# Linear attention and a low-rank mixer: two normalisations placed ahead of a low-rank product, and a value cast moved to GpSimd

## The chip, the cores and the metric

The kernel runs on one core of one Trainium2 chip. The metric is the device time of one execution in microseconds (us), given as the median of several executions. Of each kernel one execution is also recorded by the hardware profiler. The profile's own clock starts at the first instruction that it records, and all times of day below ("at 29.16") are counted from there.

## What is computed

The reference takes q, k and v of 8 batches, 8 heads, 576 positions and 64 features per head. It applies linear attention and then a mixer to each batch:

```python
r = np.maximum(x, 0.0)                                   # phi, for q and k
phi = np.concatenate([r * c, r * s], axis=-1)            # c, s: cos and sin of the position
kv  = np.einsum('bhsf,bhsd->bhfd', k_p, v)
z   = np.sum(k_p, axis=2)
x   = np.einsum('bhsf,bhfd->bhsd', q_p, kv) / (np.einsum('bhsf,bhf->bhs', q_p, z)[..., None] + 1e-06)
# heads are put side by side: x is (8, 576, 512)
h   = x.transpose(0, 2, 1) @ U @ V                       # over positions, rank 32
u   = x + h.transpose(0, 2, 1)
out = u + np.maximum(u @ w_ch1, 0.0) @ w_ch2             # 512 -> 2048 -> 512
```

Inputs and outputs are float32; the kernel multiplies in bf16 and accumulates in float32.

## The kernel before

**Tiling.** The 576 positions of a batch are five chunks: chunks 0 to 3 have 128 positions each, in an interleaved order (row p of chunk c is position 4p + c), and chunk 4, the "tail", has the last 64. Two batches share one 128-row tail tile. The order `ORD` (line 562) is tail first: 4, 0, 1, 2, 3.

**Stages of a batch.** `q_prep` and `k_prep` (lines 225 and 231) make the cosine and the sine half of phi, one instruction each for a chunk; the engine of each half is an argument. `qtr_unit` (258) transposes phi(q) on TensorE. `v_prep` and `v_block` (191 and 202) cast v into `v_ext`, which has a column of ones behind each head so that one product gives kv and z. `kv_unit` (237) makes kv of four heads: for each head, one matmul for each of the five chunks, and then a cast. `den_unit` (299) makes the reciprocals of the denominators of four heads, and `xh_unit` (315) the normalised attention of four heads in one chunk: four matmuls and then one multiplication on VectorE that releases the accumulator. `A_unit` (359) makes A = transposed x times U, `u_unit` (375) makes u of one chunk, and `uTd_open`, `uTd_mm` and `uTd_evac` (411 to 434) make the transposed u of 128 features directly: four matmuls with the identity open the accumulator, one matmul "V.A" adds h, and a cast stores it as `uT`. `g1_main` (456) makes one of 16 hidden blocks (four matmuls and a ReLU on ScalarE), and `g2_part` (500) a quarter of an output chunk.

**What sets the order.** The schedule is written by hand (line 57): each engine executes its own instructions in the order in which the program names them, and waits only through semaphores. From line 735 on a list of slots, the hidden and output blocks, is emitted one after the other. `at(j, ...)` (708) hangs more work behind slot j. Batch 0 and batch 1 are written out by hand instead of through `attention_plan`. For them `chain_head` (619) goes from v to the normalised attention of heads 0 to 3, `chain_mid` (636) makes heads 4 to 7, opens the transposed u of features 0 to 255 and completes it (this half needs heads 0 to 3 alone), and `chain_end` (659) does the other 256 features. For batch 0, `fill(n)` is a number of idle "keep-warm" matmuls on zeros (`warm0`, 664). For batch 1, `fill1` (723) puts hidden blocks 8 to 12 and two u chunks of batch 0 in between. Batch 1's chains hang behind slot 7, and its q and k preparation behind slots 0 to 6.

**Buffers.** The accumulators are in PSUM under tags. "o" has two buffers, "g" three, "X" and "T" one each. A new tile waits until the tile that had its buffer has been read. `xt` and `xt1` name the tag of each `xh_unit`: in batch 1 all five use "o", and so do both `u_unit` calls of `fill1`.

**Queues.** All loads of q, k and v go out on SP's queue. The weights go out on POOL's, where they stand in order with POOL's own casts: w1 in quarters of four hidden blocks (`w1_load`, 89), the second at line 684, the third and fourth after slot 2, and w2 in four parts after slot 6. A tiny copy to `mark` ahead of a weight load holds POOL until its source is there: line 717 until batch 1's q tail is transposed, line 719 until the first half of batch 1's v has landed. Line 642 does the like for SP, whose loads for batch 2 follow.

In the head of batch 1, v of heads 0 to 3 is cast by VectorE in three instructions and v of heads 4 to 7 by ScalarE in two.

Of the kernel before, what the change touches and what calls it, by code (L numbers as in the profile page):

```python
# [17 lines left out]
def kernel(  # L18
# [14 lines left out]
    H = 8  # L33
# [9 lines left out]
    TS = 64  # L43
# [5 lines left out]
    def tail(b):  # L49
        lo = TS * (b % 2)  # L50
        return slice(lo, lo + TS)
# [8 lines left out]
    kst, vst, qst, kt, vt, qt = {}, {}, {}, {}, {}, {}  # L60
# [40 lines left out]
    def cast(eng, o, i):  # L101
        if eng is nc.scalar:
            nc.scalar.activation(out=o, in_=i, func=AF.Copy, bias=0.0, scale=1.0)  # L103
        else:
            eng.tensor_copy(out=o, in_=i)  # L105


    V_, A_, G_ = nc.vector, nc.scalar, nc.gpsimd
# [9 lines left out]
        out=iota[:, 0:4], pattern=[[1, 4]], base=0, channel_multiplier=4,  # L118
        allow_small_or_imprecise_dtypes=True,
    )  # L120
    for lo in (0, TS):
        nc.gpsimd.iota(
            out=iota[lo : lo + TS, 4:5], pattern=[[1, 1]], base=512, channel_multiplier=1,
# [11 lines left out]
        out=stU[:, 0:4, :], in_=moe_U[0:512, :].rearrange("(p c) r -> p c r", c=4)  # L135
# [33 lines left out]
    def keep_warm(n, tag, bufs):  # L169
        w_ps = ps.tile([P, 512], FP32, tag=tag, bufs=bufs, name="w_ps")  # L170
        for _ in range(n):
            nc.tensor.matmul(out=w_ps, lhsT=zero[:, 0:P], rhs=zero, start=True, stop=True)  # L172
# [3 lines left out]
    mark = const.tile([TS, 1], FP32)  # L176
# [14 lines left out]
    def v_prep(b, h0=0, h1=H, cs=range(5), engs=None):  # L191
        vx = v_ext[b % 2]
        for n, c in enumerate(cs):
            eng = engs[n] if engs else G_
            if eng is None:
                continue
            if c < 4:
                cast(eng, vx[:, c, h0:h1, 0:D], vst[b][:, h0:h1, c, :])
            else:
                cast(eng, vx[tail(b), 4, h0:h1, 0:D], vt[b][tail(b), h0:h1, :])  # L200

    def v_block(b, h0, h1, c0, c1, eng):
        cast(
            eng,
            v_ext[b % 2][:, c0:c1, h0:h1, 0:D].rearrange("p c h d -> p h c d"),
            vst[b][:, h0:h1, c0:c1, :],
        )
# [29 lines left out]
    def kv_unit(b, hg, tag, bufs, eng=None):  # L237
        if b not in kv_sb:
            kv_sb[b] = pool.tile([P, H, E], BF16, tag="kv", bufs=2, name="kv")
        acc = ps.tile([P, 4, E], FP32, tag=tag, bufs=bufs, name="kv_ps")  # L240
        vx = v_ext[b % 2]
        for i in range(4):
            h = hg * 4 + i
            for c in range(5):
                nc.tensor.matmul(  # L245
                    out=acc[:, i, :],
                    lhsT=k_p[b][:, c, h, :] if c < 4 else k_tl[:, h, :],
                    rhs=vx[:, c, h, :],
                    start=(c == 0),
                    stop=(c == 4),  # L250
                )
        cast(eng or V_, kv_sb[b][:, hg * 4 : hg * 4 + 4, :], acc)
# [32 lines left out]
    def qT_of(b, c, h):  # L285
        return q_pT[b][:, c, h, :] if c < 4 else q_tlT[:, h, :]

    def x_alloc(b):
        if b not in x_bf:
            x_bf[b] = pool.tile([P, 4, DM], BF16, tag="x_bf", bufs=2, name="x_bf")  # L290

    def x_of(b, c, rows=slice(0, P)):
        return x_bf[b][:, c, :] if c < 4 else x_tl[rows, :]
# [21 lines left out]
    def xh_unit(b, c, h0, h1, rec, tag, bufs):  # L315
        x_alloc(b)
        n = h1 - h0
        rows = slice(0, P) if c < 4 else tail(b)
        acc = ps.tile([P, n, D], FP32, tag=tag, bufs=bufs, name="xh_ps")
        for h in range(h0, h1):  # L320
            nc.tensor.matmul(
                out=acc[:, h - h0, :], lhsT=qT_of(b, c, h), rhs=kv_sb[b][:, h, 0:D],
                start=True, stop=True,
            )
        nc.vector.tensor_tensor(
            out=x_of(b, c, rows)[:, h0 * D : h1 * D].rearrange("p (i d) -> p i d", d=D),
            in0=acc[rows],
            in1=rec[rows, c, :].unsqueeze(2).to_broadcast([P if c < 4 else TS, n, D]),
            op=ALU.mult,
        )  # L330
# [25 lines left out]
    def U_of(b, c):  # L356
        return U_bf[:, c if c < 4 else 4 + b % 2, :]

    def A_unit(b, tag, bufs, eng=None, n0=0, n1=DM, a_ps=None):
        if b not in A_sb:  # L360
            A_sb[b] = pool.tile([P, DM], BF16, tag="A_sb", bufs=2, name="A_sb")
        if a_ps is None:
            a_ps = ps.tile([P, DM], FP32, tag=tag, bufs=bufs, name="a_ps")
        for c in range(5):
            nc.tensor.matmul(  # L365
                out=a_ps[:, n0:n1],
                lhsT=U_of(b, c),
                rhs=x_of(b, c)[:, n0:n1],
                start=(c == 0),
                stop=(c == 4),  # L370
            )
        cast(eng or V_, A_sb[b][:, n0:n1], a_ps[:, n0:n1])
        return a_ps

    def u_unit(b, c, tag, bufs):
        if b not in u_bf:
            u_bf[b] = pool.tile([P, 4, DM], BF16, tag="u_bf", bufs=3, name="u_bf")
            if b % 2 == 0:
                u_tl[b // 2] = pool.tile([P, DM], BF16, tag="u_tl", bufs=2, name="u_tl")
        rows = slice(0, P) if c < 4 else tail(b)  # L380
        va = ps.tile([P, DM], FP32, tag=tag, bufs=bufs, name="va_ps")
        nc.tensor.matmul(out=va, lhsT=V_bf[:, c, :], rhs=A_sb[b], start=True, stop=True)  # L382
        nc.vector.tensor_tensor(  # L383
            out=u_bf[b][:, c, :] if c < 4 else u_tl[b // 2][rows, :],
            in0=x_of(b, c, rows),
            in1=va[rows, :],
            op=ALU.add,
        )
# [37 lines left out]
    def uTd_evac(b, d, eng):  # L426
        cast(eng, uT[b][:, :, d, :], uT_ps[b, d])

    def uTd_mm(b, d):
        t = uT_ps[b, d]  # L430
        nc.tensor.matmul(
            out=t.rearrange("m c t -> m (c t)"), lhsT=A_sb[b][:, d * P : d * P + P],
            rhs=V_bf[:, 0:4, :].rearrange("r c t -> r (c t)"), start=False, stop=True,
        )
# [127 lines left out]
    ORD = (4, 0, 1, 2, 3)  # L562
# [53 lines left out]
    TL = (0, 1, 2, 3, 4)  # L616
    O2, G3 = ("o", 2), ("g", 3)

    def chain_head(b, fill, xt, engs):
        v_prep(b, 0, 4, (4,), (engs[0],))  # L620
        v_block(b, 0, 4, 0, 3, V_)
        v_block(b, 0, 4, 3, 4, engs[0])
        kv_unit(b, 0, "T", 1)
        fill(0)
        rec0 = den_unit(b, 0, 4, "X", 1)
        v_prep(b, 4, 8, (4,), (A_,))
        v_block(b, 4, 8, 0, 4, A_)
        fill(1)
        for n, c in enumerate(ORD):
            xh_unit(b, c, 0, 4, rec0, *xt[n])  # L630
            if n == 1:
                fill(2)
            if n == 3:
                kv_unit(b, 1, "T", 1, A_)

    def chain_mid(b, fill, xt, dt):
        fill(3)
        m = 3 if b == 0 else 2
        rec1 = den_unit(b, 4, 8, *dt)
        if b == 1:  # L640

            nc.sync.dma_start(out=mark2, in_=rec1[0:1, 0, 0:1])
        for n, c in enumerate(ORD[:m]):
            xh_unit(b, c, 4, 8, rec1, *xt[n])
        u01 = ps.tile([P, 2, 512], FP32, tag="X", bufs=1, name="u01")
        uTd_open(b, 0, None, None, u01[:, 0, :].rearrange("p (c t) -> p c t", c=4))
        uTd_open(b, 1, None, None, u01[:, 1, :].rearrange("p (c t) -> p c t", c=4))
        a0 = A_unit(b, "T", 1, A_, 0, 256)
        fill(4)
        uTd_mm(b, 0)  # L650
        uTd_mm(b, 1)
        uTd_evac(b, 0, A_)
        uTd_evac(b, 1, A_)
        for n, c in enumerate(ORD[m:]):
            xh_unit(b, c, 4, 8, rec1, *xt[m + n])
        fill(5)
        return a0

# [21 lines left out]
    G_.tensor_copy(out=mark, in_=kt[0][0:TS, 0, 0:1])  # L680
    w1_load(0)
    cast_uv()
    chain_head(0, warm0, (O2, O2, G3, G3, O2), (A_,))
    w1_load(1)
    alloc_q(1)
    load_main(qst[1], q, 1)
# [21 lines left out]
    def at(j, *thunks):  # L708
        beside.setdefault(j, []).extend(thunks)
# [6 lines left out]
        at((4, 5, 5, 6, 6)[n], lambda c=c, n=n: k_prep(1, c, (V_, A_)))  # L716
    at(2, lambda: G_.tensor_copy(out=mark, in_=q_tlT[0:TS, 0, TS : TS + 1]))
    at(2, lambda: [w1_load(2), w1_load(3)])
    at(6, lambda: G_.tensor_copy(out=mark, in_=vst[1][0:TS, 0, 0, 0:1]))
    at(6, lambda: [w2_load(n) for n in range(4)])  # L720
    st1 = {}

    def fill1(n):
        if n in (0, 4):
            u_unit(0, 4 if n == 0 else 0, "o", 2)
        if n > 0:
            g1_main(0, 7 + n)

    xt1 = (O2, O2, O2, O2, O2)
    at(7, lambda: chain_head(1, fill1, xt1, (V_,)))  # L730
    at(7, lambda: st1.update(a=chain_mid(1, fill1, xt1, ("T", 1))))
    at(7, lambda: chain_end(1, st1["a"]))
    at(13, lambda: uTd_close(1, 2, V_), lambda: uTd_close(1, 3, A_))
# [2 lines left out]
    for pr in range(NPAIR):  # L736
        e, o = 2 * pr, 2 * pr + 1
# [57 lines left out]
```

## Time and profile before

| | us |
|---|---|
| median of 4 runs | 332.02 |
| lowest and highest of them | 330.39, 334.46 |
| the profiled execution's own time | 331.94 |
| its span, from first to last instruction | 330.2 |
| TensorE busy | 315.5 |
| ScalarE busy | 163.6 |
| VectorE busy | 152.2 |
| GpSimd busy | 30.3 |

The span is what the profile shows, and the 1.7 us between it and the execution's own time lie around it. The mean granted clock of TensorE is 0.999 of full speed. In the profile PE is TensorE, PEld its weight loads, DVE VectorE, ACT ScalarE, POOL GpSimd and SP the engine that issues most loads. A row of the timeline gives start, length, engine, line, operation, tiles and count; the bracket at its end is the time for which the engine stood idle before it and what ended that idle time. Matmuls overlap: one of 512 columns lasts 0.38, but the next starts 0.216 after it, so the cost of a matmul to TensorE is read from start to start. A row with a count merges several instructions.

### The profile page before, as it was taken

How to read it: one execution, taken by the hardware profiler on the slowest of the kernel's cores; microseconds unless marked ns; L12 is line 12 of the kernel's file. 1: busy time of each engine (PE TensorE's matmuls, PEld its weight loads, DVE VectorE, ACT ScalarE, POOL GpSimd, SP SyncE). 2: the span in 40 equal slices, each digit the busy share in tenths (PEclk: the TensorE clock that was granted, in tenths of full speed). 3: DMA queues.
4: the chain of work that ended last, by engine and by line, in shares of the span. 5: the costliest groups of instructions: out<-in, count | busy, mean ns of one | idle time of the engine just before them, and what ended most of it. 6: DMA issues, size and time to landing. Idle time of an engine off the chain costs nothing.

```text
span 330.2 us, 5833 instructions
## 1 busy us (share of the span) xinstructions
PE 315.5 (96%) x2422; PEld 169.1 (51%) x2422; DVE 152.2 (46%) x334; ACT 163.6 (50%) x272; POOL 30.3 (9%) x61
## 2 busy tenths in 40 slices
PE   8899799999889799999999999999999999999995
PEld 3565564485455344556455444556455444464443
DVE  7668754834656951154726940345626610001211
ACT  4828755786819226565900766556700067650000
POOL 1224203001011100000111010000112100000000
PEclk9999999999999999999999999999999999999999
DMA  7999999966344128960499479801552230001131
GB/s 233 272 275 271 207 256 327 283 204 233 106 146 116 46 79 187 238 214 11 115 226 363 150 202 247 268 2 41 151 144 66 79 95 2 0 2 64 64 97 64
DMA packets 79052, 50.73 MB, mean 154 GB/s; under 512 B 47186, under 2 KB 76242, under 8 KB 79026
## 3 DMA queue, kind: packets, MB, share of 16 engines
q1 hardware_dynamic: 72594, 39.09, 42.5%
q0 software_dynamic: 6432, 11.27, 13.5%
q8 instruction: 19, 0.31, 0.4%
q14 instruction: 7, 0.06, 0.1%
HBM read 36.86 MB, written 9.44 MB: 140 GB/s over the span
## 4 chain that ended last, share of the span: by engine, by line
PE 66%; DVE 5%; issue 1%; ACT 1%; DVEq 0%
PE o_ps L518 30%; PE g_ps L466 25%; PE gt_ps L486 3%; PE va_ps L382 2%; PE kv_ps L245 2%; PE x_ps L339 2%; DVE k_p L213 2%; PE a_ps L365 2%; DVE o_sb L528 1%; PE t_ps L262 1%; DVE k_tl L213 1%; DVE rec L297 0%; ACT k_p L211 0%; DVE x_bf L349 0%; DVE rec L296 0%
## 5 line engine op out<-in xcount | busy, mean ns | idle before, releaser
L466 PE MATMUL g_ps<-uT,w_bf 128*128 128x512 bf16 x512 | 118.5, 379 | 0.6 <-DMA w_bf<-in_moe_w_ch_dram 0.6
L518 PE MATMUL o_ps<-w_bf,hid 128*128 128x512 bf16 (+1 forms) x528 | 118.2, 372 | 0.5 <-DVE o_sb L528 0.5
L475 ACT ACTIVATE hid<-g_ps 128x512 bf16<-128x512 f32 x128 | 76.2, 596 | 83.3 <-PE g_ps L466 83.3
L518 PEld LDWEIGHTS <-hid 128*128 128x128 bf16 x528 | 49.9, 98 | 53.6 <-issue 1.6
L466 PEld LDWEIGHTS <-w_bf 128*128 128x128 bf16 x512 | 48.4, 98 | 55.0 <-DMA w_bf<-in_moe_w_ch_dram 0.8
L528 DVE TENSOR_TENSOR o_sb<-u_bf,o_ps 128x512 f32<-128x512 bf16 (+1 forms) x33 | 22.0, 668 | 67.9 <-PE o_ps L518 67.8
L538 POOL DMA_DIRECT2D out_dram<-o_sb x24 | 13.4, 557 | 177.9 <-DVE o_sb L528 160.8
L383 DVE TENSOR_TENSOR u_bf<-x_bf,va_ps 128x512 bf16<-128x512 bf16 x32 | 21.9, 686 | 10.2 <-PE va_ps L382 10.2
L105 DVE CAST kv<-kv_ps 128x260 bf16<-128x260 f32 x14 | 6.0, 428 | 37.1 <-PE kv_ps L245 37.1
L211 ACT ACTIVATE q_p<-qst,sinw 128x512 bf16<-128x512 f32 x29 | 20.4, 710 | 4.0 <-DMA qst<-in_q_dram 3.9
L349 DVE TENSOR_TENSOR x_bf<-x_ps,rec 128x512 bf16<-128x512 f32 x24 | 16.6, 691 | 0.8
L103 ACT ACTIVATE v_ext<-vst 128x512 bf16<-128x512 f32 (+2 forms) x23 | 14.8, 653 | 2.7 <-DMA vst<-in_v_dram 2.6
L486 PE MATMUL gt_ps<-uT_tl,w_bf 128*128 128x128 bf16 x256 | 16.1, 219 | 0.0
L486 PEld LDWEIGHTS <-w_bf 128*128 128x128 bf16 x256 | 15.1, 98 | 1.4
L382 PE MATMUL va_ps<-A_sb,V_bf 128*128 128x512 bf16 x40 | 15.2, 379 | 0.3 <-DVE A_sb L105 0.3
L518 PE MATMUL o_ps<-w_bf,hid_tl 128*128 128x512 bf16 x64 | 15.4, 379 | 0.0
L245 PEld LDWEIGHTS <-k_p 128*128 128x128 bf16 x256 | 11.3, 97 | 6.1 <-ACT k_p L211 2.0
L245 PE MATMUL kv_ps<-v_ext,k_p 128*128 128x65 bf16 x256 | 12.0, 193 | 2.4 <-DVE v_ext L105 2.4
L172 PE MATMUL w_ps<-zero 128*128 128x512 bf16 x40 | 11.9, 433 | 1.8 <-DVE halfpi L142 1.2
L213 DVE TENSOR_SCALAR k_p<-kst,cosw 128x512 bf16<-128x512 f32 x28 | 13.1, 484 | 1.0 <-DMA kst<-in_k_dram 0.9
L339 PEld LDWEIGHTS <-q_pT 128*128 128x128 bf16 x192 | 9.1, 98 | 8.2 <-DVE x_bf L349 1.6
L296 DVE TENSOR_SCALAR rec<-x_ps 128x8 f32<-128x8 f32 (+1 forms) x30 | 4.9, 164 | 17.0 <-PE x_ps L339 16.9
(100 smaller groups left out, 262.0 us busy)
## 6 DMA issues: line engine op xcount, KB each, us to landing
qst<-in_q_dram SPq DMA_DIRECT2D x8, 1024.0 KB, 9.1
kst<-in_k_dram SPq DMA_DIRECT2D x8, 1024.0 KB, 7.8
vst<-in_v_dram SPq DMA_DIRECT2D x6, 1024.0 KB, 9.5
out_dram<-o_sb POOLq DMA_DIRECT2D x24, 256.0 KB, 2.7
w_bf<-in_moe_w_ch_dram POOLq DMA_DIRECT2D x8, 512.0 KB, 10.1
vst<-in_v_dram SPq DMA_DIRECT2D x4, 512.0 KB, 8.2
out_dram<-o_sb SPq DMA_DIRECT2D x7, 256.0 KB, 2.3
qt<-in_q_dram SPq DMA_DIRECT2D x8, 128.0 KB, 8.0
```

Of the source, the lines that this page charges most:

```text
L211: nc.scalar.activation(out=o, in_=i, func=AF.Relu, bias=0.0, scale=w)
L213: eng.tensor_scalar(out=o, in0=i, scalar1=0.0, scalar2=w, op0=ALU.max, op1=ALU.mult)
L245: nc.tensor.matmul(out=acc[:, i, :], lhsT=k_p[b][:, c, h, :] if c < 4 else k_tl[:, h, :], rhs=vx[:, c, h, :], start=(c == 0), stop=(c == 4),)
L339: nc.tensor.matmul(out=acc[:, g, i * E : i * E + E], lhsT=qT_of(b, c, h), rhs=kv_sb[b][:, h, :], start=True, stop=True,)
L349: nc.vector.tensor_tensor(out=x_of(b, c, rows).rearrange("p (g i d) -> p g i d", g=2, d=D), in0=view[:, :, :, 0:D], in1=rec[rows].unsqueez ...
L382: nc.tensor.matmul(out=va, lhsT=V_bf[:, c, :], rhs=A_sb[b], start=True, stop=True)
L383: nc.vector.tensor_tensor(out=u_bf[b][:, c, :] if c < 4 else u_tl[b // 2][rows, :], in0=x_of(b, c, rows), in1=va[rows, :], op=ALU.add,)
L466: nc.tensor.matmul(out=g_ps.rearrange("p (c t) -> p c t", c=4), lhsT=w1_bf[:, d, j * P : j * P + P], rhs=uT[b][:, :, d, :], start=(d == 0) ...
L475: nc.scalar.activation(out=hid[b][:, j, :], in_=g_ps, func=AF.Relu, bias=0.0, scale=1.0)
L486: nc.tensor.matmul(out=g_ps[:, jj, :], lhsT=w1_bf[:, d, j * P : j * P + P], rhs=uT_tl[pr][:, d, :], start=(d == 0), stop=(d == 3),)
L518: nc.tensor.matmul(out=o[:, cols], lhsT=lhs[:, j, c * P : c * P + P], rhs=w2_bf[:, j, cols], start=(j == 0), stop=(j == NJ - 1),)
L528: nc.vector.tensor_tensor(out=o_sb[:, cols], in0=u[:, cols], in1=o[:, cols], op=ALU.add)
```

## The change

There are four edits. In `chain_mid`, two of the remaining `xh_unit` calls (chunks 2 and 3 in batch 0, where m is 3, and chunks 1 and 2 in batch 1, where m is 2) are emitted ahead of `fill(4)` and of the two V.A products, and the rest stay behind them. In batch 0 the second evacuation of transposed u goes from ScalarE to VectorE. In batch 1, v of heads 0 to 3 and the whole v tail are cast by GpSimd, behind the weight loads of slot 2, and the copy to `mark` at line 719 goes. The `u_unit` of `fill1(4)` takes a "g" buffer instead of an "o" buffer, and two keep-warm matmuls come ahead of batch 1's head.

```diff
-    def chain_head(b, fill, xt, engs):
-        v_prep(b, 0, 4, (4,), (engs[0],))
-        v_block(b, 0, 4, 0, 3, V_)
-        v_block(b, 0, 4, 3, 4, engs[0])
+    def chain_head(b, fill, xt):
+        if b == 0:
+            v_prep(b, 0, 4, (4,), (A_,))
+            v_block(b, 0, 4, 0, 3, V_)
+            v_block(b, 0, 4, 3, 4, A_)
         kv_unit(b, 0, "T", 1)
         fill(0)
         rec0 = den_unit(b, 0, 4, "X", 1)
-        v_prep(b, 4, 8, (4,), (A_,))
+        if b == 0:
+            v_prep(b, 4, 8, (4,), (A_,))
         v_block(b, 4, 8, 0, 4, A_)
...
         a0 = A_unit(b, "T", 1, A_, 0, 256)
+        for n in (m, m + 1):
+            xh_unit(b, ORD[n], 4, 8, rec1, *xt[n])
         fill(4)
         uTd_mm(b, 0)
         uTd_mm(b, 1)
         uTd_evac(b, 0, A_)
-        uTd_evac(b, 1, A_)
-        for n, c in enumerate(ORD[m:]):
-            xh_unit(b, c, 4, 8, rec1, *xt[m + n])
+        uTd_evac(b, 1, V_ if b == 0 else A_)
+        for n in range(m + 2, 5):
+            xh_unit(b, ORD[n], 4, 8, rec1, *xt[n])
         fill(5)
...
-    chain_head(0, warm0, (O2, O2, G3, G3, O2), (A_,))
+    chain_head(0, warm0, (O2, O2, G3, G3, O2))
...
     at(2, lambda: [w1_load(2), w1_load(3)])
-    at(6, lambda: G_.tensor_copy(out=mark, in_=vst[1][0:TS, 0, 0, 0:1]))
+    at(2, lambda: v_prep(1, 0, H, (4,), (G_,)))
+    at(2, lambda: v_block(1, 0, 4, 0, 4, G_))
     at(6, lambda: [w2_load(n) for n in range(4)])
...
         if n in (0, 4):
-            u_unit(0, 4 if n == 0 else 0, "o", 2)
+            u_unit(0, 4 if n == 0 else 0, *(O2 if n == 0 else G3))
...
-    at(7, lambda: chain_head(1, fill1, xt1, (V_,)))
+    at(7, lambda: keep_warm(2, "X", 1))
+    at(7, lambda: chain_head(1, fill1, xt1))
```

## The prediction, made before the result

> **What bounds the kernel now.** I read the page first, then the timeline of 16 to 48 us, the only stretch that the diff touches, and last the waits of TensorE behind it.
>
> ```profile
> PE 315.5 (96%) x2422; PEld 169.1 (51%) x2422; DVE 152.2 (46%) x334; ACT 163.6 (50%) x272; POOL 30.3 (9%) x61
> ```
>
> TensorE is busy for 96% of the span; 14.7 us are left in all (330.2 - 315.5). The edit removes no matmul (it adds two idle ones), so it can only gain where TensorE waits inside the stretch. The timeline of TensorE alone, columns start, length, engine, line, operation, tile, count, wait before it:
>
> ```profile
> 20.89 0.60 PE L431 MATMUL u<-V_bf,A_sb 128*128 128x512 bf16 x2 [0.26 <-ACT A_sb L103]
> 21.34 0.42 PE L321 MATMUL xh_ps<-kv,q_pT 128*128 128x64 bf16 x8
> ...
> 22.02 0.72 PE L365 MATMUL a_ps<-x_bf,U_bf 128*128 128x256 bf16 x4
> ...
> 29.16 1.04 PE L466 MATMUL g_ps<-uT,w_bf 128*128 128x512 bf16 x4 [0.64 <-DMA w_bf<-in_moe_w_ch_dram]
> ```
>
> Three things: V.A waits for the cast of A (20.89); the last two normalisations of batch 0 follow it; and at 29.16 TensorE waits for weights. That is the second quarter of w1 (hidden block 4 is the first to read it), issued at 17.91, with its last piece landing at 29.10 in the trace. Then the start of batch 1:
>
> ```profile
> 33.94 1.32 ACT L211 ACTIVATE k_p<-kst,sinw 128x512 bf16<-128x512 f32 x2
> 34.46 0.96 DVE L105 CAST v_ext<-vst 128x768 bf16<-128x768 f32 x2
> ...
> 35.18 0.49 PE L245 MATMUL kv_ps<-v_ext,k_p 128*128 128x65 bf16 x4 [1.50 <-DVE v_ext L105]
> ```
>
> The reader is to see two ends close together: VectorE's v casts end at 35.42 (34.46 + 0.96) and ScalarE's sine halves of k at 35.26 (33.94 + 1.32; single record 35.25). The wait of 1.50 is put down to the first, but the second is nearly as late. Last, batch 1's first half of features:
>
> ```profile
> 42.73 0.42 DVE L325 TENSOR_TENSOR x_bf<-xh_ps,rec 128x256 bf16<-128x256 f32 x1
> 42.76 0.38 PE L382 MATMUL va_ps<-A_sb,V_bf 128*128 128x512 bf16 x1
> ...
> 44.59 1.22 DVE L325 TENSOR_TENSOR x_bf<-xh_ps,rec 128x256 bf16<-128x256 f32 x3 [0.74 <-PE xh_ps L321]
> 45.07 0.29 PE L321 MATMUL xh_ps<-kv,q_pT 128*128 128x64 bf16 x4 [0.39 <-DVE x_bf L325]
> ...
> 46.05 0.60 PE L365 MATMUL a_ps<-x_bf,U_bf 128*128 128x256 bf16 x4
> ```
>
> The third head product at 45.07 needs one of the two "o" buffers and waits until a normalisation frees it. From 45.2 to about 87 TensorE runs without such waits; the later ones (89.5, 93, 112, 116 us) are queues of ACT and DVE that were themselves fed by TensorE, with no DMA named. So what is gained at 45 should reach the end one for one.
>
> **Batch 0, moved normalisations.** Two groups of 4 head products (the x8 at 21.34, 0.25 us of issue) go into the gap before V.A. A's last matmul issues at 20.15, then the products to 20.5, one idle matmul to 20.72; V.A still waits for the A cast and stays at 20.89. Behind it the products' 0.25 is gone. Their "o" and "g" buffers are free (the tail's normalisation ends at 20.08). VectorE, free at 20.74, does the two normalisations at 0.38 each by 21.5, so A's second half no longer waits between its chunks 2 and 3 (0.23 between those two issues where 0.11 is normal: 0.12). Gain here 0.25 + 0.12 = **0.37**. The second uT evacuation moves from ScalarE (0.59) to VectorE (0.69, the row at 23.98), 21.54 to 22.23; behind it VectorE has A's second cast, ready only at about 22.6, so nothing waits. TensorE reads uT at about 22.75, when the first w1 quarter (landed 22.21) is in too.
>
> But this 0.37 ends at 29.16. The w1 quarter comes at 29.10 whatever TensorE did: its issue at 17.91 stands before the edited code, so 0.64 becomes about 1.0. I book **0**; its other end is the full -0.37, if that landing were not last. One thing starts earlier: the mark that reads q_tlT and the w1 quarters 3 and 4 behind it on POOL's queue, 27.22 to about 26.85. They are first needed at 37.17, so no gain; they can take bandwidth from batch 1's k and v, at most those 0.37. VectorE's k_tl waits for kt until 29.91, and 0.28 follows before it is next needed: 0 to +0.1, I take 0.
>
> **Batch 1, v on GpSimd.** Off VectorE: three casts, 33.83 to 35.42. Off ScalarE: the tail's second half (0.42 at 35.76), after kv has begun, 0 on the path. On POOL, behind w1's issues (end 28.92): the 64x512 tail and one 128x1024 block, in place of a 0.39 mark.
>
> ```profile
> 31.54 0.39 POOL L719 COPY mark<-vst 64x1 f32<-64x1 f32 x1 [2.62 <-DMA vst<-in_v_dram]
> 31.99 3.34 POOL L97 DMA_DIRECT2D w_bf<-in_moe_w_ch_dram  x4
> ...
> 55.51 2.29 POOL L105 CAST v_ext<-vst 128x512 bf16<-128x512 f32 x4 [2.30 <-DMA vst<-in_v_dram]
> ```
>
> The tail lands at 30.41 and costs 0.61 (row at 52.59), to 31.06. The first half of v lands at 31.42; by the last line 512 elements cost 0.57 back to back, so 1024 cost 1.15: 31.5 to about 32.7. The Trainium skill, "GPSIMD Engine Reference", section 3.1, gives 1.8 cycles per element at 1.2 GHz, which would make 1.54 and 33.1. Either end is ahead of TensorE, which comes at 33.51. Behind the cast on POOL wait only the four w2 issues: 31.99 becomes about 32.7, landing from about 41 and not read before 71.
>
> So the wait goes over to ScalarE, not away. In the record, kv's chunk 3 loaded its weights at 35.30, right after k's last sine (35.25), and its matmul issued at 35.47, after the last v cast. Now it issues at about 35.33: **-0.14**. It cannot be more, since ScalarE runs without a gap from 30.23, when it got hidden block 4, that is from the w1 landing: 0.60, k_tl 0.72, hidden 5, two sines, hidden 6, two sines. The two keep-warm matmuls (0.43) lie in TensorE's gap from 33.51 to 35.33; without it they would cost 0.43.
>
> **A rule against this part.** VectorE makes k's cosines while POOL casts:
>
> ```profile
> 31.40 0.88 DVE L213 TENSOR_SCALAR k_p<-kst,cosw 128x512 bf16<-128x512 f32 x2
> ```
>
> That is 0.40 from start to start for 512 elements. The Trainium skill, "SBUF — State Buffer", section "Who interferes with whom", says that tensor_scalar, copy and cast on VectorE can run in a mode that takes a port pair shared with GpSimd, and that whoever is second stands still for the whole instruction. Nothing in this trace has a POOL cast beside such an instruction; beside POOL's w2 issues one cosine took 0.61 in place of 0.48. By the row, VectorE loses about 0.13; by the rule up to the cast's 1.15. Cosines end at 33.80, so 35.0 at worst, still ahead of 35.25: the sum is the same by both, 0. The cover is 1.45 us.
>
> **Batch 1, moved normalisations.** After A's first half (last issue 42.64, next slot 42.755) come the products of chunks 1 and 2. Chunk 1 takes the buffer of the tail, normalised by 42.70: it issues at 42.77 to 42.89. Chunk 2 takes that of chunk 0, normalised until 43.15: it issues at 43.21. A **new wait** of 0.33, with u's first V.A, hidden block 11 and the two V.A of features queued behind it. The old one goes: 8 products from 44.26 end their issue at 44.51, the next came at 45.07, so 0.56 saved; chunk 3 now meets a buffer freed at 43.6. A's second half starts at 46.05 - 0.56 + 0.35 (0.33 and two hand-overs of 0.01) = 45.84, and chunk 3's normalisation ends at about 45.6. u moves to the "g" buffers: VectorE frees that one at about 44.7, wanted at 47. ScalarE's hidden block 11 and both evacuations come 0.6 later, 46.3 at the last; the uT tile is read at about 50. Gain **0.21**; ends 0.1 and 0.35, as the new wait is longer by one VectorE step or half gone.
>
> **Sum.** -0.14 - 0.21 = -0.35, against the profiled execution's own 331.94 us (span 330.2 and 1.7 around it): 331.59, so **331.6 us**. That execution is 0.08 below the median 332.02; the four runs lie between 330.39 and 334.46, so this gain is smaller than their spread. About 1% (3.3 us) is what a measurement of this kernel can tell from no change.
>
> **Rivals.**
> B: batch 0 counts as well, because w1's second quarter is in before TensorE asks for it. For: most of its pieces land by 27.3, only stragglers at 28.15 and 29.10. Against: 0.64 of wait in this record. Then 331.6 - 0.4 = 331.2.
> C: the batch 1 move does nothing; the buffer wait only changes its place, 0.56 against 0.56, if chunk 2's product waits for one more normalisation. For: two "o" buffers stay two. Against: chunk 0's normalisation is already running when it is asked for. 331.94 - 0.14 = 331.8.
> D, on the other side: the port pair at the cosines. If POOL's tail (0.61) and block (1.15) both stop VectorE, and w2's issues slow the last two cosines by 0.13 to 0.3 each, the last ends at 33.80 + 1.76 + 0.5 = 36.1, and kv's chunk 3 issues 0.65 later than now: 331.94 + 0.65 - 0.21 = 332.4. It decides once VectorE slips by 1.9 us (35.47 + 0.21 - 33.80). For: POOL's cast and the cosines start within 0.1 of each other. Against: the tail's cast ends before the first cosine.
>
> **How the numbers follow.** Likeliest (A) 0.50, B 0.17, C 0.13, D 0.12, something that this profile does not show 0.08 (of it 0.03 beyond 1% faster, 0.05 beyond 1% slower). A's own range, with the ends of its terms and the medians' scatter, is 331.0 to 332.3. B to D lie between 331.2 and 332.4; with some 0.8 of scatter of such a median on either side the range is 330.4 to 333.1. All four cases are within 1%: faster 0.04, same 0.90, slower 0.06.
>
> **What would show it.** Right, if: kv_ps of batch 1 waits for ScalarE's k_p or VectorE's, no longer for a v_ext cast, and its fourth matmul comes 0.1 to 0.2 earlier relative to the w1 landing; the w_bf wait grows from 0.64 to about 1.0; TensorE shows a wait of about 0.3 for x_bf before u's V.A and none before chunk 3; POOL's cast of 1024 takes 1.1 to 1.6. Wrong, if: the w_bf wait stays or goes (B), cosines of over 1 us stand beside POOL's cast (D), or anything after 50 us changes by more than its shift.

## The result and the profile after

| | before | changed |
|---|---|---|
| median, us | 331.92 (64 executions) | 330.75 (43) |
| lowest and highest | 330.27, 335.87 | 329.48, 334.03 |
| span of the profiled execution | 330.2 | 328.2 |

The ratio is 0.9962, 95% interval 0.9947 to 0.9976: 0.8 to 1.8 us less, 1.3 at the middle. The forecast was 0.35 less. The sign was right, and the time lies inside the stated range, but that is owed to the width of the range (330.4 to 333.1, with the scatter of a median in it): the gain is more than three times the forecast. So the question is where the other 0.9 us comes from. A first hint is that the gain is not even. A tenth of the executions lie below 330.43 before and below 329.78 after, 0.65 less; a tenth lie above 333.90 before and above 331.75 after, 2.15 less.

The two records alone do not answer it. Their spans differ by 2.0, of which 0.6 is there at the first "A" of batch 0 (20.15 against 19.56), ahead of every edit: the first loads came earlier in that execution. From there on I compare distances. The busy times of the page of the changed kernel are nearly those of before:

```profile
PE 315.2 (96%) x2424; PEld 169.4 (52%) x2424; DVE 151.9 (46%) x332; ACT 162.2 (49%) x270; POOL 31.2 (10%) x62
```

TensorE at the end of batch 0, in the changed kernel's timeline:

```profile
19.56 0.27 PE L365 MATMUL a_ps<-x_tl,U_bf 128*128 128x256 bf16 x1
19.67 0.41 PE L321 MATMUL xh_ps<-kv,q_pT 128*128 128x64 bf16 x8
...
20.31 0.61 PE L431 MATMUL u<-V_bf,A_sb 128*128 128x512 bf16 x2
...
21.18 0.60 PE L365 MATMUL a_ps<-x_bf,U_bf 128*128 128x256 bf16 x4
...
21.73 0.61 PE L417 MATMUL uT_ps<-ident,x_bf 128*128 128x128 bf16 x8
...
27.46 1.03 PE L466 MATMUL g_ps<-uT,w_bf 128*128 128x512 bf16 x4
```

and the first and the last of these places before:

```profile
20.15 0.27 PE L365 MATMUL a_ps<-x_tl,U_bf 128*128 128x256 bf16 x1
...
22.69 0.61 PE L417 MATMUL uT_ps<-ident,x_bf 128*128 128x128 bf16 x8
```

The eight products stand ahead of V.A. From V.A to A's second half it is 0.87 (20.31 to 21.18), where it was 1.13. From the last matmul of A's first half to the opening of the next accumulators it is 2.17 (19.56 to 21.73), where it was 2.54: 0.37 less. The wait for w1's second quarter, 0.64 before, is not there at 27.46: in this execution the quarter had landed by 27.1. Then the start of batch 1, all engines:

```profile
30.33 1.72 DVE L213 TENSOR_SCALAR k_p<-kst,cosw 128x512 bf16<-128x512 f32 x2
...
30.72 1.05 POOL L105 CAST v_ext<-vst 128x1024 bf16<-128x1024 f32 x1 [0.46 <-DMA vst<-in_v_dram]
...
32.23 1.32 ACT L211 ACTIVATE k_p<-kst,sinw 128x512 bf16<-128x512 f32 x2
...
32.57 1.00 DVE L213 TENSOR_SCALAR k_p<-kst,cosw 128x512 bf16<-128x512 f32 x2
...
33.18 0.19 PE L245 MATMUL kv_ps<-v_ext,k_p 128*128 128x65 bf16 x1 [0.71 <-DVE k_p L213]
33.45 0.58 ACT L475 ACTIVATE hid<-g_ps 128x512 bf16<-128x512 f32 x1
33.68 0.10 PEld L245 LDWEIGHTS <-k_p 128*128 128x128 bf16 x1 [0.44 <-ACT k_p L211]
33.71 0.19 PE L245 MATMUL kv_ps<-v_ext,k_p 128*128 128x65 bf16 x1 [0.34 <-DVE k_p L213]
```

kv now waits for k alone: VectorE's cosines end at 33.57 and ScalarE's sines at 33.55, nearly at the same moment. And two cosines took 1.72 together while GpSimd cast, where they took 0.88 before. Last, TensorE at batch 1's first half of features:

```profile
40.99 0.29 PE L321 MATMUL xh_ps<-kv,q_pT 128*128 128x64 bf16 x4
41.45 0.29 PE L321 MATMUL xh_ps<-kv,q_pT 128*128 128x64 bf16 x4 [0.17 <-DVE x_bf L325]
41.57 0.38 PE L382 MATMUL va_ps<-A_sb,V_bf 128*128 128x512 bf16 x1
41.79 1.02 PE L466 MATMUL g_ps<-uT,w_bf 128*128 128x512 bf16 x4
42.65 0.59 PE L431 MATMUL u<-V_bf,A_sb 128*128 128x512 bf16 x2
43.08 0.29 PE L321 MATMUL xh_ps<-kv,q_pT 128*128 128x64 bf16 x4
```

The new wait is there (40.99 + 0.13 of issue to 41.45: 0.33, as forecast), and the old one, at the third product (43.08), is gone.

### The profile page after: what moved, and what is told of

Same layout as the page of the kernel before. It is cut to its first block, busy times and chain, and to the rows that moved or that the text cites. A ratio compares the mean times of both kernels' runs of the same rounds, so it can differ in the third digit from the quotient of the medians.

```text
span 328.2 us, 5835 instructions
## 1 busy us (share of the span) xinstructions
PE 315.2 (96%) x2424; PEld 169.4 (52%) x2424; DVE 151.9 (46%) x332; ACT 162.2 (49%) x270; POOL 31.2 (10%) x62
## 4 chain that ended last, share of the span: by engine, by line
PE 67%; DVE 5%; issue 1%; ACT 1%; DVEq 0%
PE o_ps L518 30%; PE g_ps L466 25%; PE gt_ps L486 3%; PE va_ps L382 2%; PE kv_ps L245 2%; PE x_ps L339 2%; DVE k_p L213 2%; PE a_ps L365 2%; DVE o_sb L528 1%; PE t_ps L262 1%; DVE k_tl L213 1%; DVE rec L297 0%; ACT k_p L211 0%; DVE x_bf L349 0%; DVE rec L296 0%
## 5 line engine op out<-in xcount | busy, mean ns | idle before, releaser
L213 DVE TENSOR_SCALAR k_p<-kst,cosw 128x512 bf16<-128x512 f32 x28 | 14.1, 517 | 0.1
L262 PE MATMUL t_ps<-ident,q_p 128*128 128x128 bf16 x128 | 9.6, 219 | 3.4 <-ACT q_tlT L103 1.6
```

Source lines behind the costliest of these rows:

```text
L213: eng.tensor_scalar(out=o, in0=i, scalar1=0.0, scalar2=w, op0=ALU.max, op1=ALU.mult)
```

## The experiments

My first theory after the result, T, was that the wait for w1 belongs to some executions only, and that without it VectorE's v casts end well behind ScalarE's sines, so that moving them is worth 0.5 or more. Its rivals were R, the prediction's own sum, and S, that the gain sits in executions with late loads. These letters are not those of the prediction's rivals. Each part was then run alone. "Before" stands for the kernel before on the same chip.

**The v cast alone** (e1: all edits for batch 1's v and the two keep-warm matmuls, `chain_mid` as before).

```diff
+        if b == 0:
+            v_prep(b, 0, 4, (4,), (A_,))
...
-    at(6, lambda: G_.tensor_copy(out=mark, in_=vst[1][0:TS, 0, 0, 0:1]))
+    at(2, lambda: v_prep(1, 0, H, (4,), (G_,)))
+    at(2, lambda: v_block(1, 0, 4, 0, 4, G_))
...
+    at(7, lambda: keep_warm(2, "X", 1))
```

> Only batch 1's v cast moves to GpSimd (with the keep-warm pair). Theory T (the wait for w1's second quarter at 29.16 belongs to some executions only; without it VectorE's k cosines and v casts, not ScalarE's sines, end last before batch 1's kv): -0.5 to -0.65 us, so a median near 331.3, and in the profile VectorE ends its cosines no more than 0.2 before or after the sines. Rival R (the record of before is typical, ScalarE's sines end last): -0.14, near 331.8. Rival S (the gain sits in executions whose v lands late): nearly the whole -1.2, mostly in the slow half of the runs.

Median 331.73 against 332.39, ratio 0.9968 (0.9948 to 0.9987). Most of the whole gain is here, and R's 0.14 is outside the interval (0.4 to 1.7 less). In its record the sines end last (34.55), the cosines 0.33 earlier. The middle, 1.06, is more than T's 0.5 to 0.65, but T's size is inside the interval.

**Batch 0's part alone** (e2).

```diff
+        early = 2 if b == 0 else 0
+        for n in range(m, m + early):
+            xh_unit(b, ORD[n], 4, 8, rec1, *xt[n])
         fill(4)
         uTd_mm(b, 0)
         uTd_mm(b, 1)
         uTd_evac(b, 0, A_)
-        uTd_evac(b, 1, A_)
-        for n, c in enumerate(ORD[m:]):
-            xh_unit(b, c, 4, 8, rec1, *xt[m + n])
+        uTd_evac(b, 1, V_ if b == 0 and early else A_)
+        for n in range(m + early, 5):
+            xh_unit(b, ORD[n], 4, 8, rec1, *xt[n])
```

> Only batch 0's two normalisations go ahead of V.A, with the second evacuation on VectorE. T: -0.31 where TensorE does not wait for w1's second quarter, 0 where it does, so -0.1 to -0.31; the profile shows A's second half 0.3 to 0.4 earlier relative to A's first half. R: 0, the w1 wait grows by what was gained. S: 0.

Ratio 0.9997 (0.9962 to 1.0031): no gain seen, as R had it. Its record shows where the gain went, first on TensorE:

```profile
28.83 1.04 PE L466 MATMUL g_ps<-uT,w_bf 128*128 128x512 bf16 x4 [1.03 <-DMA w_bf<-in_moe_w_ch_dram]
```

and then on VectorE, in the same record:

```profile
30.49 0.49 DVE L213 TENSOR_SCALAR k_tl<-kt,cosw 64x512 bf16<-64x512 f32 x1 [1.96 <-DMA kt<-in_k_dram]
```

The wait for w1 is 1.03 in place of 0.64, longer by about the 0.37 that was gained, and behind it VectorE waits 1.96 for k's tail.

**Batch 1's part alone** (e3: as e2, with this instead).

```diff
+        early = 2 if b == 1 else 0
...
-            u_unit(0, 4 if n == 0 else 0, "o", 2)
+            u_unit(0, 4 if n == 0 else 0, *(O2 if n == 0 else G3))
```

> Only batch 1's two normalisations go ahead of V.A, with u of batch 0 in a g buffer. T, R and S alike: -0.21, with a new wait of about 0.2 to 0.3 for x_bf ahead of u's product and none ahead of the third head product.

Ratio 0.999 (0.9958 to 1.0021), too wide for 0.2. The records decide: from kv's fourth matmul in batch 1 to the end of the span it is 294.70, 294.72, 294.70, 294.75 and 294.74 us in the five records without this edit (before, e1, e4, f2, f4), and 294.49 to 294.54 in the seven with it and without a fall of the clock (the changed kernel, e3, k2, k3, e6, f6, f1). That is 0.20 less, and each group lies within 0.05.

**No wait for w1** (e4: the kernel before, but hidden blocks 4 to 7 of batch 0 read w1's first quarter, so those values are not the reference's; the loads stay).

```diff
-                lhsT=w1_bf[:, d, j * P : j * P + P],
+                lhsT=w1_bf[:, d, (j % 4 if b == 0 and 4 <= j < 8 else j) * P :][:, 0:P],
```

> The kernel before, with hidden blocks 4 to 7 of batch 0 reading w1's first quarter in place of the second (their values are not the reference's); all loads stay. This takes the w1 wait away. R: TensorE is up to 0.6 earlier at block 4, but VectorE's casts then end last, so -0.2 to -0.4. T: the wait is rare, so the median moves by less than 0.2, and the profile shows kv's fourth matmul waiting for v_ext by about 0.6 more than for k_p.

Ratio 1.0015 (0.9987 to 1.0043). The wait for w1 was 0.64 in the record of before and is found in ten of the fourteen records of all kernels (0.23 to 1.11), but no gain is seen from taking it away. The record shows one reason: VectorE and ScalarE then wait for k's tail, until 29.93, where VectorE started on it at 29.91 before. So a gain ahead of this point has two loads to pass. The median is not clean, though, as the table below shows: without the wait more executions lose their clock, and those without such a loss (330.85 against 331.12, 8 and 26 executions) leave room for a small gain. T's first half falls (the wait is not rare); its second half stands: in this record the v casts end at 34.83 and the sines at 34.33.

**What the record of e2 showed.** Its granted clock was not 1. Two stretches of its trace follow; the columns are start and end, length, the busy time and count of PE, PEld, DVE, ACT and POOL, the granted clock, the DMA share and GB/s:

```profile
32.40:35.80 3.40, 1.50 (x18) 0.71 (x17) 2.98 (x7) 3.38 (x7) 3.35 (x5) 0.99 1.23 214
35.80:39.20 3.40, 2.88 (x39) 1.72 (x37) 1.56 (x4) 1.14 (x2) 0.28 (x1) 0.50 1.24 206
```

and the same two stretches of the kernel before:

```profile
32.40:35.80 3.40, 1.85 (x20) 0.96 (x19) 2.96 (x6) 3.38 (x7) 2.93 (x4) 1.00 1.24 208
35.80:39.20 3.40, 3.10 (x52) 1.87 (x49) 2.29 (x6) 2.06 (x3) 0.00 (x0) 1.00 1.24 206
```

For 3.4 us, right at batch 1's kv, TensorE ran at half its clock. The hidden block there, four matmuls, shows it:

```profile
37.45 1.86 PE L466 MATMUL g_ps<-uT,w_bf 128*128 128x512 bf16 x4
```

It took 1.86 in place of 1.02. Over a span of 330 us, 3.4 us at half make a mean clock of 0.995, and the mean clock is listed for every execution. So each kernel has a share of executions with such a fall, which I count as a mean under 0.9965 (profiled executions are in the counts):

| kernel | with a fall | median without | median with |
|---|---|---|---|
| before (three chips) | 74 of 129 | 331.12, 330.90, 331.74 | 333.15, 332.81, 333.56 |
| changed | 7 of 44 | 330.45 | 331.62 |
| e1, v cast and two keep-warm | 5 of 22 | 331.40 | 332.41 |
| e2, batch 0 only | 8 of 14 | 331.08 | 333.00 |
| e3, batch 1 only | 6 of 14 | 330.79 | 332.98 |
| e4, no wait for w1 | 14 of 22 | 330.85 | 334.06 |

A mean of 0.990 or less is two falls or more: 8 of e4's 22, and 7 of the 59 of before on its chip. In e1 the executions without a fall are no faster than those of before on its chip (331.40 against 331.12). Its gain is in the slow part of the executions, where falls and, by S, late loads both are.

That made theory C (of the clock; not the prediction's rival C): TensorE's gap ahead of batch 1's kv makes the clock fall, and the two keep-warm matmuls, which I had booked at nothing, prevent it.

**The two matmuls alone, and all but them** (k1: the kernel before with this one line; k2: the changed kernel without it).

```diff
+    at(7, lambda: keep_warm(2, "X", 1))
     at(7, lambda: chain_head(1, fill1, xt1, (V_,)))
```

> The kernel before with nothing but the two keep-warm matmuls ahead of batch 1's head. Theory C (clock: TensorE's gap before batch 1's kv, 1.5 to 2.3 us, makes its granted clock fall to half for 3.4 us in about half of the executions of before, at some 2 us each; the two matmuls prevent most of this): the share of executions with a mean clock under 0.9965 falls from about 0.56 (33 of 59) to 0.2 to 0.3, and the median by 0.5 to 1.0 us; executions at full clock are not changed. Rival T (VectorE's v casts end last, and the clock has no part): 0, the matmuls lie in a gap.

> The changed kernel without the two keep-warm matmuls. C: the share of executions under 0.9965 rises from 0.16 (7 of 44) to 0.4 or more, and the median rises by 0.4 to 0.8 us against the changed kernel, so a ratio to before of about 0.998 to 0.999. T: no change, the ratio stays near 0.996.

k1: 6 of 12 with a fall, ratio 0.9995 (0.9961 to 1.0028). k2: 6 of 12, ratio 0.9979 (0.995 to 1.0009). C as I had put it is half wrong: the two matmuls do not do it in the kernel before. The record of k1 shows why, TensorE:

```profile
33.12 0.38 PE L172 MATMUL w_ps<-zero 128*128 128x512 bf16 x1
34.87 0.49 PE L245 MATMUL kv_ps<-v_ext,k_p 128*128 128x65 bf16 x4 [1.37 <-DVE v_ext L105]
...
36.90 1.87 PE L466 MATMUL g_ps<-uT,w_bf 128*128 128x512 bf16 x4
```

1.37 us of the gap stay empty, another 0.30 before the denominators, and the clock falls at 36.5. In the changed kernel the rest of the gap is broken up, since v is there early and kv's first two matmuls run at 32.24. But k2 says that this too is not enough without the two matmuls, if 6 of 12 is not chance: with both, it is 7 of 44 (changed), 5 of 22 (e1) and 4 of 10 (e6, below).

**Five keep-warm matmuls in the changed kernel** (k3).

```diff
-    at(7, lambda: keep_warm(2, "X", 1))
+    at(7, lambda: keep_warm(5, "X", 1))
```

> The changed kernel with five keep-warm matmuls in place of two (0.65 us more of issue, inside a gap that lasts from 31.8 to 33.7 in the record). C: no or nearly no execution under 0.9965, the slow half of the runs goes, median 0 to 0.3 below the changed kernel, ratio about 0.995. T: no change, or up to 0.2 slower where the gap is short.

No execution of 12 with a fall, all means 0.998 or more; median 330.17, ratio 0.9944 (0.9913 to 0.9974). As C expected. k2 ran on the same chip and differs by these five matmuls alone: 331.47 there, 1.3 more, with 6 of 12. Not all of that is the clock, since k2's six executions without a fall (median 331.12) are slower than k3's too.

**The cast in four pieces** (e6).

```diff
-    at(2, lambda: v_block(1, 0, 4, 0, 4, G_))
+    at(2, lambda: [v_block(1, 0, 4, c, c + 1, G_) for c in range(4)])
```

> The changed kernel with GpSimd's cast of 1024 elements as four casts of 256, one for each chunk. If the shared port pair is what made two of VectorE's k cosines take 1.72 us together in place of 0.88 (they ran beside GpSimd's cast), each of the short casts can hold it for some 0.3 us only: the two take 1.0 to 1.5, no single one over 0.9. The time stays within 0.3 us of the changed kernel, since ScalarE's sines end at the same point.

```profile
30.84 1.06 DVE L213 TENSOR_SCALAR k_p<-kst,cosw 128x512 bf16<-128x512 f32 x2
...
31.22 1.62 POOL L105 CAST v_ext<-vst 128x256 bf16<-128x256 f32 x4 [0.46 <-DMA vst<-in_v_dram]
...
32.42 1.34 DVE L213 TENSOR_SCALAR k_p<-kst,cosw 128x512 bf16<-128x512 f32 x2
```

The same two cosines took 1.06, and GpSimd 1.62 in place of 1.05. The other two, the first of which still met the last pieces, took 1.34 in place of 1.00. All four together took 2.40 here, 2.72 beside the one long cast and 1.88 in the kernel before, so shorter GpSimd instructions took away 0.32 of the 0.84 that the cosines lost. Ratio 0.9969 (0.9935 to 1.0002), 4 of 10 with a fall; the sines end last (34.00), so nothing was to be gained.

**Five matmuls under each part.** With the clock held, the parts can be compared without it: f2 is the kernel before with five, f4 the v cast with five, f6 both moves of normalisations with v as before and five.

In f2:

```diff
+    at(7, lambda: keep_warm(5, "X", 1))
     at(7, lambda: chain_head(1, fill1, xt1, (V_,)))
```

In f4, against e1:

```diff
-    at(7, lambda: keep_warm(2, "X", 1))
+    at(7, lambda: keep_warm(5, "X", 1))
```

In f6, f2's line, e3's `u_unit`, and e2's loop for both batches:

```diff
+        early = 2
```

> The kernel before with five keep-warm matmuls ahead of batch 1's head (1.1 us of issue in a gap of 1.6 or more), and nothing else. Theory C2 (it takes enough of them to keep the clock up; two did not in the kernel before, 6 of 12): no more than 2 in 10 executions under 0.9965, median near the 331.0 of before's own full-clock executions, ratio 0.996 to 0.997. Rival (the clock falls because of the waits for w1 and k before the gap, and not of the gap): share stays near 0.5, ratio 0.999 to 1.000.

> Only batch 1's v cast on GpSimd, with five keep-warm matmuls. C2: no more than 1 in 10 under 0.9965. Against the kernel before with five, what is left is the v cast alone at full clock: 0.1 to 0.6 us less if VectorE's casts were the last to end, 0 if the shared port gives back what they cost.

> Both moves of normalisations ahead of V.A (batch 0 and batch 1), v cast as before, with five keep-warm matmuls. Against the kernel before with five: 0.2 us less from batch 1 and 0 to 0.3 from batch 0, so a ratio to before of about 0.995 to 0.996.

| kernel | with a fall | median | ratio to before |
|---|---|---|---|
| f2 | 0 of 12 | 332.47 | 0.9987 (0.9963 to 1.001) |
| f4 | 1 of 12 | 331.86 | 0.9979 (0.9954 to 1.0003) |
| f6 | 1 of 12 | 331.62 | 0.9967 (0.9939 to 0.9994) |
| f1, below | 0 of 12 | 331.00 | 0.9943 (0.9921 to 0.9964) |

The share is settled: five idle matmuls in a gap that exists anyway take it from 21 of 35 on this chip (74 of 129 on all three) to 0 of 12. The worth in time is not: f2 came down by 0.3 in place of the expected 1.0 to 1.3, and its interval includes no change. Its median lies 0.7 above those executions of before on this chip that kept their clock by themselves (331.74). That would follow if these were the ones whose loads came early and whose gap was short, but no run here shows it. Its record had a late k tail; ScalarE's sines and VectorE's casts behind it:

```profile
31.41 0.49 DVE L213 TENSOR_SCALAR k_tl<-kt,cosw 64x512 bf16<-64x512 f32 x1 [1.97 <-DMA kt<-in_k_dram]
...
34.55 1.32 ACT L211 ACTIVATE k_p<-kst,sinw 128x512 bf16<-128x512 f32 x2
...
35.86 0.96 DVE L105 CAST v_ext<-vst 128x768 bf16<-128x768 f32 x2
```

k's tail came 1.5 later than in the record of before, the sines ended at 35.87, and the v casts at 36.82: here they cost 0.95. f4 against f2, the v cast at full clock, is 0.6 less; f6 against f2 is 0.85 less, where 0.2 to 0.5 was expected. The intervals of f4 and of f6 overlap that of f2: with 12 executions each, this does not tell 0.3 from 0.8.

**A further version** (f1: five matmuls, and k's chunks all prepared behind slot 5).

```diff
-        at((4, 5, 5, 6, 6)[n], lambda c=c, n=n: k_prep(1, c, (V_, A_)))
+        at((4, 5, 5, 5, 5)[n], lambda c=c, n=n: k_prep(1, c, (V_, A_)))
```

> The changed kernel with five keep-warm matmuls and all of k's chunks 0 to 3 prepared behind slot 5, so that ScalarE's last two sines no longer stand behind hidden block 6. ScalarE then ends its sines 0.57 earlier and VectorE's cosines (held up by the port pair for about 0.8) end last: kv 0.1 to 0.5 us earlier than with five keep-warm matmuls alone, so a ratio to before of 0.993 to 0.9945, and no execution under 0.9965.

Ratio 0.9943, the same as k3's 0.9944 on another chip: no gain seen from the order of the sines. If that order is worth nothing, f1 against f2, on one chip, is all of the change with the clock held on both sides: 331.00 against 332.47, 1.5 less, as much as the whole gain. In f1's record hidden block 4 waited for w1 again (0.53) and the four sines ran on from 31.23 to 33.79, with the cosines at 33.71. Both k3 and f1 lie below the changed kernel's 0.9962, on other chips and with intervals that overlap its own.

## Why the prediction was right in sign and wrong in size

**Batch 0, moved normalisations: booked 0, not refuted.** The 0.37 was made (0.37 in the record by the opening of the next accumulators, 0.32 of it kept at the V.A products that follow). Alone it gave 0.9997, with an interval of over 1 us either way. The step named one load that swallows it, w1 at 29.10. There are two: in e4's record, without the first, k's tail holds the engines to the same point. Whether some of it comes through in other executions stays open; f6 leaves room for it.

**Batch 1, moved normalisations: booked 0.21, measured 0.20.** Every piece of that step holds: the new wait of 0.33, the old one gone, the "g" buffer free in time.

**v on GpSimd: booked 0.14, about 0.4 by an estimate from the records.** The step said "It cannot be more, since ScalarE runs without a gap from 30.23". That is true of one execution. How far the v casts end behind the sines in the seven records that cast v on VectorE is 0.16 (before), 0.51 (e2), 0.11 (e3), 0.50 (e4), 0.47 (k1), 0.95 (f2) and 0.12 (f6), mean 0.40. The lag is smallest with the earliest k tail (29.02 in e3) and largest with the latest (31.39 in f2), but in between it is 0.47 with 29.72 (k1) and 0.12 with 29.80 (f6), so k's landing is not all of it. The term was read off one record of a quantity that changes from execution to execution. The two runs that differ in it alone with the clock held, f2 and f4, are 0.6 apart, with intervals that overlap.

**The clock: booked at nothing.** I wrote that the two matmuls "lie in TensorE's gap" and asked what they cost, not what the gap costs. The profile of before showed a granted clock of 0.999, so the clock had no part in the sum, and that is the term that was missing. The pair alone does not change the share (k1, 6 of 12), and the other edits without it do not either (k2, 6 of 12); together they do (7 of 44). More than half of the executions of before have the fall; the profiled one was of the others. A fall costs 1.1 to 1.45 in the records (kv's fourth matmul to the end 295.81 in e2 and 296.16 in k1, against 294.71). The share went from 0.57 to 0.16, so by an estimate from these figures this is worth about 0.4 x 1.3 = 0.5. The executions with a fall are 1.8 to 2.0 longer in before, more than one fall costs in the records. Later loads in them would account for the rest; no run shows the loads of more than one execution of a kernel.

**The sum again:** 0.5 for the clock, 0.4 for the v cast, 0.2 for batch 1, 0 to 0.3 for batch 0: 1.1 to 1.4, against 1.3 measured (0.8 to 1.8). It fits, but only the 0.2 is measured by itself. That the change lowers the share of falls is shown; what this is worth in time is worked out from three records and two shares. The runs with the clock held on both sides speak for less of it: f2 is only 0.3 below before, and f1 against f2 has 1.5 of gain with the clock held, where this sum leaves 0.6 to 0.9. So S, that the gain sits in executions with late loads, is not excluded, and how the 0.9 us divides between the clock and the v cast stays open.

**The rule against the part was right.** The row had suggested 0.13 on VectorE, the Trainium skill ("SBUF — State Buffer", "Who interferes with whom") up to the whole cast. Two cosines took 0.84 more (1.72 for 0.88) beside one cast of 1.05, 1.67 in k3, and 1.06 when the cast was cut in four. It was rightly booked at 0, but the cover was thinner than the 1.45 stated: the cosines ended 0.02 behind the sines. GpSimd's 1024 elements took 1.05, and 1.04 to 1.34 in the six records with this cast, around the row's 1.15 and under the 1.54 worked out from the Trainium skill, "GPSIMD Engine Reference", section 3.1.

**The rivals and the signs.** B (331.2) was the nearest by its number. Its sign, no wait for w1, is there in the record of the changed kernel, but 0.4 from batch 0 is not shown. The prediction's C is excluded by the 0.20. D did not decide: cosines of over 1 us stand beside GpSimd's cast, but VectorE slipped by 0.84, not 1.9. Of the signs of being right, the waits at kv and at batch 1's first half came as stated. kv's fourth matmul did not come earlier relative to w1's landing (6.59 behind it, 6.37 before), since in this execution w1 was not the load that was waited for.

## What to carry to other kernels

Before costing an edit from one record, list the mean granted clock of every execution: a kernel whose record shows 0.999 may lose its clock in more than half of the others, and a few idle matmuls in a gap can prevent it. What that saves has to be measured, not read off the share. A term that is the difference of two engines' ends behind a load ("A ends 0.16 after B") needs several records, since it changes with the load. A gain made ahead of such a load can be swallowed until every load at that point is early enough, not only the one that the wait names.

## What the runs showed of the hardware

The clock fell to half for 3.41 us in the traces of e2 and k1, and came back by itself. In the list of clock states that each trace holds, every state between two changes lasts a whole number of times 3.413 us: 30.72 ahead of the fall (nine), 3.41 for the fall, 293.55 behind it in e2 (86), 290.13 in k1 (85), and one state of 324.27 in before (95). So the clock changed here only at points that lie 3.413 apart, and these points lie elsewhere in each execution. The stretch between two of them that came ahead of the fall had TensorE busy for 1.51 us in e2 and for 1.63 in k1 (33.04 to 36.45). In e2:

```profile
32.35:35.76 3.41, 1.51 (x17) 0.72 (x16) 3.03 (x7) 3.39 (x7) 3.36 (x5) 1.00 1.23 214
```

e4 kept its clock, although one stretch of this length was emptier (first row). Its points, at 30.57, 33.99 and 37.40, cut that stretch in two (second and third row):

```profile
32.32:35.73 3.41, 0.92 (x20) 0.79 (x22) 2.58 (x7) 3.36 (x7) 3.15 (x4) 1.00 1.24 209
30.57:33.99 3.42, 1.74 (x9) 0.59 (x6) 3.33 (x8) 3.37 (x7) 2.13 (x4) 1.00 1.22 239
33.99:37.40 3.41, 2.25 (x44) 1.68 (x46) 2.31 (x6) 2.32 (x4) 1.48 (x2) 1.00 1.24 207
```

The same holds for e3 (1.26 in its emptiest stretch, 1.78 and 2.89 between its points) and for before (1.55; 1.87 and 3.11). So whether a gap costs a fall depends also on where these points lie in that execution, which would make it differ between executions with equal loads. A threshold does not follow: at the end of f2 a stretch with 1.51 busy (326.67 to 330.08) was followed by another at full clock.

The Trainium skill, "TensorE: Matmul & The Clock Gate", Part 1, speaks of an idle window of about 3.4 us. The length agrees with the traces, but TensorE need not be idle for all of it: the longest single gap in such a stretch was 1.84 us in e2 and 1.37 in k1. Idle matmuls on zeros count as activity here: five of them kept the mean clock at 0.998 or more in 34 of 36 executions of f2, f4 and f6, and in all 24 of k3 and f1.
